# Ten of fourteen hidden tiles of a gated MLP's first half put on a seven-product scheme, with partial sums kept on chip and a new order of all steps

## The chip, the cores and the metric

The kernel runs on one core of a Trainium2 chip. The metric is the device time of one execution in microseconds; several executions of the same program are timed and their median is given. The core's engines run side by side, each through its own instructions in order: PE (the matrix engine), DVE and ACT (element-wise work, DVE on two tensors, ACT on one), POOL (here it issues transfers that add to what is already there) and SP (it issues the other transfers). Transfers run on 16 DMA engines. Matmuls write to PSUM, eight banks of 128 x 512 fp32 values.

## The reference

All tensors are fp32. x has 2048 rows of 512.

```python
def _A_ref(x, w_r, w_i):                       # a spectral filter
    X = rfft2(x)                               # over rows and columns
    return irfft2(X * (w_r + 1j * w_i))
def _B_ref(x, w1, b1, w2, b2):                 # an MLP, 512 -> 1792 -> 512
    h = gelu(einsum("bsd,df->bsf", x, w1) + b1)
    return einsum("bsf,fd->bsd", h, w2) + b2
g = sigmoid((x * gate_w).sum(-1, keepdims=True))
out = g * _A_ref(x, ...) + (1 - g) * _B_ref(x, ...)
```

## The kernel before

**The MLP** is cut into 14 tiles f of 128 hidden columns and four chunks c of 512 rows. The chunks 0 and 1 are the first half (`CA`, letter A in the new code), 2 and 3 the second half (`CB`, B). Each fp32 operand is split into a high part and a low part (ACT copies the rounded high part, DVE subtracts it), and a product is three fast matmuls: high by high, high by low, low by high. So a tile (f, c) takes 4 x 3 = 12 matmuls of 512 columns for its first product, and 4 x 3 for its second (four output tiles q).

- The first half is done by `mlp(p, c)`, plainly: `ph` (12 matmuls into one bank), gelu by ACT in the bank, `split` into `g..h` and `g..l` (ACT copy, DVE difference), then `down` and `keep`.
- The second half is done by `fast(p)` with a seven-product scheme (Winograd's form of Strassen's): two f tiles by two chunks, each with its K of 512 cut in two, would be eight products of six matmuls; it takes seven (42 matmuls in place of 48 for two f and two c). It needs sums of weight halves (`spread_w`: seven tiles `wa0h`, `wa0l`, `wash`, `wasl`, `wath`, `watl`, `wa1` for each pair u of f tiles, by ACT, DVE and one adding transfer) and sums of x halves (`early_x`, `spread_x`, `put`, `less`: seven forms), and three copies (ACT) and two sums (DVE, with `five`) between the products. Its banks are `nu` and `ux`; matmuls add onto values that ACT has copied into `ux`.
- `down` multiplies by w2 into a bank `po` (`poB`) for a group of f tiles, in three groups for the first half (`PASS_A`) and four for the second (`PASS_B`). `keep` copies each bank to SBUF by ACT and sends it to a DRAM tile `bacc[c]`: the first group with a store, the later ones with a transfer by POOL that adds in DRAM.
- w2 tiles come by `halve` (load, ACT copy, ACT negated copy, adding transfer by POOL); for f from 10 on (`KEPT`) the split tiles of the first half are stored in DRAM (`ws`) and read back in the second. The plain w1 tiles come by `load_w`.

**The filter** is a two-dimensional Fourier transform. `forward(j)`, 16 times: two DVE sums and differences, fp32 matmuls `pd` over columns (one extra column pair gives the gate's dot product, read by DVE reductions), split into `zb`, matmuls `py` into two banks, ACT copy `pys`, a DVE sum and a DVE difference, ACT copies to `y`. Then `stage1`, `filt(q0)` and `stage4` are radix-4 steps on DVE, with the filter's weights between (`wf`, its edge columns mended by a DVE instruction with `rev`). `inverse(c, h)` goes back: `sw`, `pq`, fp32 matmuls `pz`, split into `zb`, matmuls `pa` into two banks, DVE sums. For the first half it loads the partial sums from `bacc`, multiplies by the gate (`ba`), and adds them on the way out; for the second half `last` subtracts the bank of the last group from y and writes the result. The gate is spread over partitions into `gb`.

**The order.** Each step is added to a graph with the buffers that it reads and writes. `ORDER` is a list, written out, of all steps; each engine issues its own in that order, and SP's and POOL's transfers are issued in it too. `SLOTS` says which slot of SBUF or which bank each buffer takes. PSUM was in two pools of four banks (`pf`, `pm`). Steps wait for each other by semaphores where they share a buffer.

The start: ten idle matmuls on zeros (`none`) and ten small ones fill PE until the first x and w1 arrive.

Of the kernel before, what the change touches and what calls it, by code (L numbers as in the profile page):

```python
# [23 lines left out]
PASS_A = (range(0, 5), range(5, 10), range(10, 14))  # L24
PASS_B = (range(0, 4), range(4, 6), range(6, 10), range(10, 14))
# [94 lines left out]
PSUM = ("pf", "pm")  # L120

ORDER = """
# [1153 lines left out]
```

## Time and profile before

| | us |
|---|---|
| median of 3 runs | 363.61 (363.47 to 363.66) |
| the profiled execution | 364.53 |
| its span, first to last instruction | 362.6 |
| PE busy | 356.9 (98%) |
| DVE busy | 330.1 (91%) |
| ACT busy | 254.2 (70%) |
| POOL busy | 70.3 (19%) |

In the rows of the profile `L982` is a line of the kernel, the names before and after the arrow are the tile written and the tiles read, `x16` is how many, then the busy time in us and the mean of one in ns; behind the last bar stands how long the engine was idle just before and what ended that. PEld is the loading of weights into PE, which overlaps the matmuls. All matmuls but those of `fast` have the helper's line L416. The chain of waits is the work that ended last, followed back from the last instruction.

### The profile page before, as it was taken

Reading aid. Unit: us, or ns where it says so; the run is one execution under the profiler, and the core shown is the slowest. Engines: PE = TensorE matmul, PEld = TensorE weight load, DVE = VectorE, ACT = ScalarE, POOL = GpSimd, SP = SyncE. Lnnn points to the kernel's source line nnn. Section 1 sums busy time; section 2 is a strip of 40 time slices with the busy share of each in tenths; the row PEclk is TensorE's granted clock in tenths of the full one; section 3 lists DMA queues with packets and bytes.
Section 4 is the critical chain, followed back from the end, with each engine's and each line's share of the span. In section 5 each row is a group of like instructions: output and inputs, shape, how many; then the busy total and the mean of one; then the engine's idle time right before and its main releaser. Section 6 shows DMA issues by size and latency. Waiting matters only on the chain.

```text
span 362.6 us, 5730 instructions
## 1 busy us (share of the span) xinstructions
PE 356.9 (98%) x1812; PEld 303.1 (84%) x1812; DVE 330.1 (91%) x745; ACT 254.2 (70%) x471; POOL 70.3 (19%) x91
## 2 busy tenths in 40 slices
PE   8999999999999999999999999999999999999995
PEld 6888898898878788888888888888888888889885
DVE  3879999989988899999999899999988889999995
ACT  4796487989988623266566775999999988676200
POOL 1121000111021241111024420010323221113220
PEclk9999999999999999999999999999999999999999
DMA  6999868579768599998988997074869658489878
GB/s 243 339 343 210 280 200 240 115 190 211 212 131 231 135 251 182 283 297 227 266 173 136 185 142 226 32 197 104 149 104 163 111 95 177 122 207 210 210 182 244
DMA packets 46494, 70.34 MB, mean 194 GB/s; under 512 B 5376, under 2 KB 19200, under 8 KB 46464
## 3 DMA queue, kind: packets, MB, share of 16 engines
q1 hardware_dynamic: 34592, 48.93, 42.6%
q0 software_dynamic: 11440, 20.72, 37.0%
q10 hardware_dynamic: 432, 0.33, 0.3%
q8 instruction: 14, 0.23, 0.3%
q14 instruction: 16, 0.13, 0.1%
HBM read 48.32 MB, written 19.41 MB: 187 GB/s over the span
## 4 chain that ended last, share of the span: by engine, by line
PE 91%; DMA 4%; SPq 1%; ACT 1%; DVE 1%; issue 1%; DVEq 0%; ACTq 0%
PE poB L416 21%; PE po L416 20%; PE ph L416 17%; PE ux L1090 11%; PE nu L1090 8%; PE pd L416 4%; PE pz L416 4%; PE py L416 3%; PE pa L416 3%; DMA bacc<-o 3%; DMA war<-in_w 1%; ACT gb L1199 0%; SPq L877 0%; SPq L657 0%; DVE mxl L560 0%
## 5 line engine op out<-in xcount | busy, mean ns | idle before, releaser
L904 ACT ACTIVATE ph<-ph,b1t 128x512 f32<-128x512 f32 x28 | 18.3, 655 | 15.0 <-PE ph L416 15.0
L407 POOL DMA_DIRECT2D bacc<-oB x16 | 14.2, 908 | 53.5 <-ACT oB L982 52.8
L803 ACT ACTIVATE sw<-y,al 64x512 f32<-64x512 f32 x32 | 22.9, 721 | 1.2 <-DVE y L669 0.7
L407 POOL DMA_DIRECT2D bacc<-o x16 | 14.9, 993 | 41.0 <-ACT o L982 38.2
L765 DVE TENSOR_TENSOR m<-y,wf 128x514 f32<-128x514 f32 x32 | 21.5, 691 | 0.2
L982 ACT ACTIVATE o<-po 128x512 f32<-128x512 f32 x16 | 9.3, 598 | 16.8 <-PE po L416 16.8
L632 ACT ACTIVATE y<-pys 64x257 f32<-64x257 f32 x32 | 13.4, 418 | 6.4 <-DVE pys L629 5.7
L416 PEld LDWEIGHTS pz<-tg,pq 128*128 128x128 f32 x128 | 16.8, 191 | 1.2
L416 PE MATMUL pd<-cf,w 128*128 128x129 f32 x128 | 17.8, 274 | 0.0
L416 PEld LDWEIGHTS pd<-cf,w 128*128 128x128 f32 x128 | 16.8, 190 | 0.8
L1090 PE MATMUL nu<-xf,wa0h 128*128 128x512 f32 x56 | 17.5, 393 | 0.0
L416 PE MATMUL pz<-tg,pq 128*128 128x128 f32 x128 | 17.2, 274 | 0.0
L416 PE MATMUL py<-zb,tf 128*128 128x258 f32 x96 | 17.1, 294 | 0.0
L810 DVE SCALAR_TENSOR_TENSOR pq<-y,al,sw 128x256 f32<-128x256 f32 x32 | 14.8, 479 | 0.9 <-ACT sw L803 0.7
L416 PEld LDWEIGHTS py<-zb,tf 128*128 128x128 f32 x96 | 14.3, 190 | 1.1
L416 PEld LDWEIGHTS pa<-zb,ci 128*128 128x128 f32 x96 | 13.9, 188 | 1.4
L416 PE MATMUL pa<-zb,ci 128*128 128x256 f32 x96 | 14.9, 283 | 0.0
L607 DVE TENSOR_TENSOR zb<-pd,zb 128x256 fp32r<-128x256 f32 x32 | 12.7, 419 | 0.6 <-ACT zb L604 0.5
L604 ACT ACTIVATE zb<-pd 128x256 fp32r<-128x256 f32 x32 | 12.0, 384 | 1.5 <-PE py L416 0.9
L574 DVE TENSOR_TENSOR w<-eo 128x256 f32<-128x256 f32 x32 | 12.8, 419 | 0.3
L571 DVE TENSOR_TENSOR eo<-xf 128x256 f32<-128x256 f32 x32 | 12.9, 419 | 0.0
L823 DVE TENSOR_TENSOR zb<-pz,zb 128x512 fp32r<-128x512 f32 x16 | 10.9, 687 | 2.1 <-ACT zb L822 2.1
(700 smaller groups left out, 1273.4 us busy)
## 6 DMA issues: line engine op xcount, KB each, us to landing
wf<-in_wf SPq DMA_DIRECT2D x16, 257.0 KB
bacc<-o POOLq DMA_DIRECT2D x16, 256.0 KB, 6.2
bacc<-oB POOLq DMA_DIRECT2D x16, 256.0 KB, 5.0
xf<-in_xt SPq DMA_DIRECT2D x14, 256.0 KB
wr<-in_w SPq DMA_DIRECT2D x14, 256.0 KB, 4.6
tf<-tf SPq DMA_DIRECT2D x16, 192.0 KB, 4.5
bacc<-o SPq DMA_DIRECT2D x8, 256.0 KB, 5.0
ba<-bacc SPq DMA_DIRECT2D x8, 256.0 KB, 8.4
```

The source lines that it names most:

```text
L407: return add("pool", 2.3 * kb / 340, 3.4, lambda: nc.gpsimd.dma_start(dst(), src(), accum_op=ALU.add), reads, writes, rank)
L416: pe.matmul(ps, w, x, start=start, stop=stop)
L571: v(lambda s=s, op=op: vec.tensor_tensor(eo.ap()[:, s], x.ap()[:, 0:2], x.ap()[:, 2:4], op=op), 256, [x], [(eo, s)], feed)
L574: v(lambda s=s, op=op: vec.tensor_tensor(w.ap()[:, s], eo.ap()[:, :, 0], eo.ap()[:, :, 1], op=op), 256, [eo], [(w, s)], feed)
L604: a(lambda c=c: act.activation(segs(xh, c), both(c), AF.Copy), 256, [ps[c]], [(xh, c)], 0)
L607: v(lambda c=c: vec.tensor_tensor(segs(xl, c), both(c), segs(xh, c), op=ALU.subtract), 256, [ps[c], (xh, c)], [(xl, c)], 0)
L632: a(lambda o=o, i=i: act.activation(Y[j].ap()[o:o + HP, 1], pys.ap()[i:i + HP, 1], AF.Copy), 257, [(pys, 1)], [(Y[j], 1 + k)], 0, more=0.1)
L765: v(lambda mk=mk, k=k, y=y, w=w: vec.tensor_tensor(mk.ap(), y.ap(), w.ap()[:, k:k + 1, :ND].to_broadcast([P, 2, ND]), op=ALU.mult), 514, [ ...
L803: a(lambda sw=sw, y=y, o=o, i=i: act.activation(sw.ap()[o:o + HP], y.ap()[i:i + HP, ::-1, :HD], AF.Copy, scale=al.ap()[i:i + HP, 0:1]), 51 ...
L810: v(lambda sw=sw, pq_=pq_, y=y, j=j, k=k, op=op: vec.scalar_tensor_tensor(pq_.ap()[:, k], y.ap()[:, k, :HD], al.ap()[:, 1 + j:2 + j], sw.a ...
L904: a(lambda: act.activation(ps.ap(), ps.ap(), AF.Gelu_apprx_tanh, bias=b1t.ap()[:, f:f + 1]), 600, [b1t], [ps]).table = "gelu"
L1090: pe.matmul(o.ap(), w(wi, e), FX[j].ap()[:, xi, e], start=first, stop=k == 5, skip_group_check=not start)
```

## The change

- The first half's `f` 4 to 13 go by the seven-product scheme too (`seven("A", u, G)` for five pairs u); only `f` 0 to 3 stay plain (`plain`). The x of the first half is split straight into the scheme's forms (`split_x`), and `spread_x("A")` makes the other four.
- The groups of f are now four in each half: 0-3, 12-13, 4-7, 8-11 for A and 8-11, 12-13, 0-3, 4-7 for B.
- The seven weight tiles of the five pairs are stored in DRAM (`wu`, 35 stores of 256 KB) when A makes them, and B reads them back (35 loads) and doesn't make them again.
- Partial sums stay in SBUF (`SUM`, eight tiles at a time): from the second group on ACT copies the sum into the bank, the matmuls add onto it, and ACT copies it back. The adding transfers into `bacc` are gone; `bacc` is written once for A, after the gate product, and is added by POOL to the inverse's result. B's last group goes from the bank through two DVE instructions to the output.
- Both products of a `py` step, and of a `pa` step, share one bank: ACT copies the first, the second adds onto it, and DVE gets the difference as -2 x first + sum. The gate's dot products are copied out by ACT and summed once; the edge columns come ready from DRAM and are copied by ACT.
- All eight banks are one pool. `ORDER` and `SLOTS` are new throughout.

The diff, cut to what is spoken of:

```diff
-PASS_A = (range(0, 5), range(5, 10), range(10, 14))
-PASS_B = (range(0, 4), range(4, 6), range(6, 10), range(10, 14))
+GROUPS = (range(0, 4), range(12, 14), range(4, 8), range(8, 12)), (range(8, 12), range(12, 14), range(0, 4), range(4, 8))
+PLAIN = 4
...
+    wu = {u: one(f"su{u}", [P, 7, D], pool=dp, parts=7) for u in range(PLAIN // 2, NF // 2)}
...
     def forward(j):
-            v(lambda c=c, o=o: vec.tensor_reduce(o.ap()[:, n:n + 1], ps[c].ap()[:, P:P + 2], ...
+            a(lambda c=c: act.activation(logit.ap()[:, n, c], ps[c].ap()[:, P:P + 2], AF.Copy), ...
...
+        py = bank([P, 512], f"py{j}", "py")
+        for c in range(2):
+            m(lambda c=c: high(c), NE, 2, [t, (xh, c)], [py])
+            m(lambda c=c: low(c), NE, 1, [t, (xl, c)], [py])
+            o, w_ = ((lambda: pys.ap()[:, 0]), (pys, 0)) if c == 0 else ((lambda: Y[j].ap()[:, 0]), (Y[j], 0))
+            a(lambda o=o: act.activation(o(), py.ap()[:, :ND], AF.Copy), 257, [py], [w_])
+        v(lambda: vec.scalar_tensor_tensor(pys.ap()[:, 1], pys.ap()[:, 0], -2.0, py.ap()[:, :ND], op0=ALU.mult, op1=ALU.add), ...
...
+    def spread_w(s, u):
+        if s == "B" and u in wu:
+            for i, n in enumerate(TS):
+                dma(lambda i=i, n=n: raw(T[n].ap(), wu[u].ap()[:, i]), 256, [(wu[u], i)], [T[n]])
+        else:
...
+            if s == "A":
+                for i, n in enumerate(TS):
+                    dma(lambda i=i, n=n: sp.dma_start(wu[u].ap()[:, i], T[n].ap().bitcast(F32)), 256, [T[n]], [(wu[u], i)])
...
+    def down(p, c, fs, G):
+        end = p == len(GROUPS[0]) - 1
+        for q in range(NQ):
+            if p == 0:
+                SUM[c, q] = buf("w", [P, 4 * P], F32, f"s{c}{q}", cls="s")
+            o = SUM[c, q]
...
+                ps = bank([P, size], f"po{p}_{c}{q}{n.start}", "po", full=not tail, onto=p > 0)
+                if p:
+                    a(lambda ps=ps, n=n, o=o: act.activation(ps.ap(), o.ap()[:, n], AF.Copy), size, [o], [ps])
+                for f in fs:
...
+                if p == 0:
+                    a(lambda ...: act.activation(o.ap(), ps.ap(), AF.Identity, bias=b2t.ap()[:, q:q + 1]), 600, [b2t, ps], [o])
+                elif not end:
+                    copy(o, ps)
+                elif c in CA:
+                    copy(o, ps, scale=-1.0)
+                    v(... gate product on o ...)
+                    dma(... o to bacc[c] ...)
+                else:
+                    last(c, q, ps, n, tail)
+
+    def last(c, q, ps, n, tail):
+        for k, i in enumerate(some):
+            v(lambda ...: vec.scalar_tensor_tensor(t.ap()[:, s], gb..., 1.0, ps.ap()[:, s], op0=ALU.subtract, op1=ALU.mult), ...
+            v(minus_, ...)
...
...
+    def group(s, p):
+        if s == "A" and fs[0] < PLAIN:
...
+        else:
+            for u in range(fs[0] // 2, fs[-1] // 2 + 1):
+                seven(s, u, G)
```

More of the change, by code (lines that the diff above doesn't have):

```diff
@@ L332, in schedule @@
             for b in s.bufs:
-                last = held.setdefault((b.tag, b.slot), b)
-                assert last is b or last.left == 0
+                last = held.get((b.tag, b.slot))
+                assert last is b or last is None or last.left == 0
+                assert last is b or not b.onto or last.full
                 held[b.tag, b.slot] = b
@@ L418, in prods, with mm, onto, copy @@
-    def prods(ps, ah, al, bh, bl, first, last):
-        mm(ps, ah, bh, first, False)
-        mm(ps, ah, bl, False, False)
-        mm(ps, al, bh, False, last)
+    def mm(ps, w, x, start, stop, **more):
+        pe.matmul(ps, w, x, start=start, stop=stop, **more)
+    def onto(ps, w, x):
+        mm(ps, w, x, False, False, skip_group_check=True)
     def bcast(ap, *ns):
         return bass.AP(tensor=ap.tensor, offset=ap.offset, ap=[list(ap.ap[0]), *[[0, n] for n in ns], list(ap.ap[1])])
+    def copy(o, i, n=512, scale=1.0):
+        a(lambda: act.activation(o.ap(), i.ap(), AF.Copy, scale=scale), n, [i], [o])
@@ L444, in tile_kernel @@
     b1t = one("b1t", [P, NF])
-    rev = one("rev", [P, NJ, 2, 2])
-    b22 = one("b22", [P, 2, NQ], parts=2)
-    b2t, nb2 = (View(b22, i, 1, lambda t, i=i: t[:, i]) for i in range(2))
+    b2t = one("b2t", [P, NQ])
     al = one("al", [P, 1 + NJ])
-    logit = one("logit", [P, NJ], parts=NJ, pool=sa)
-    gate = one("gate", [P, NJ], parts=NJ, pool=sa)
+    logit, edges = (buf("lg", [P, NJ, 2, 2], F32, n, k, sa) for n, k in (("logit", 2 * NJ), ("edges", 1)))
+    gate = one("gate", [P, NJ], pool=sa)
     gb = buf("xhl", [P, 4, 4 * P], F32, "gb", parts=4, cls="gb")
@@ L453, in tile_kernel @@
     Y = [View(yy, 3 * j, 3, lambda t, j=j: t[:, j]) for j in range(NJ)]
-    bacc = [one(f"bacc{c}", [P, NQ, 4, P], pool=dp, parts=2 * NQ) for c in range(4)]
+    bacc = [one(f"bacc{c}", [P, NQ, 4, P], pool=dp, parts=2 * NQ) for c in CA]
     ws = {(f, k): one(f"sb{f}{k}", [P, D], pool=dp) for f in range(KEPT, NF) for k in "hl"}
+    wu = {u: one(f"su{u}", [P, 7, D], pool=dp, parts=7) for u in range(PLAIN // 2, NF // 2)}
     gsc = one("gsc", [P, NJ], pool=dp)
@@ L611, in forward, with high @@
-        py = [buf("pm", [P, 512], F32, f"py{j}{c}", pool=pp, cls="py") for c in range(2)]
+        for c in range(2):
+            v(lambda c=c: vec.tensor_tensor(segs(xl, c), both(c), segs(xh, c), op=ALU.subtract), 256, [ps[c], (xh, c)], [(xl, c)])
+            a(lambda c=c: act.activation(logit.ap()[:, n, c], ps[c].ap()[:, P:P + 2], AF.Copy), 2, [ps[c], (xh, c)], [(logit, 2 * n + c)],
+              more=0.1)
+        py = bank([P, 512], f"py{j}", "py")
         pys = t2k(f"pys{j}", cls="pys", parts=2)
-        def s_high(c):
+        def high(c):
@@ L825, in inverse, with part @@
-        ps = [buf("pf", [P, 2, 2 * P], F32, f"pa{c}{h}{ft}", pool=pp, cls="pa") for ft in range(2)]
-        def part(ft, p, z, k, first, last):
-            mm(ps[ft].ap()[:, k], CI[0].ap()[:, k, p, ft], z.ap()[:, ft, k].rearrange("p a b -> p (a b)"), first, last)
+              512, [ps, (zh, n)], [(zl, n)])
+        ps = bank([P, 2, 2 * P], f"pa{c}{h}", "pa")
+        def part(ft, p, z, k):
+            mm(ps.ap()[:, k], CI[0].ap()[:, k, p, ft], z.ap()[:, ft, k].rearrange("p a b -> p (a b)"), ft == p == k == 0 and z is zh, False,
+               skip_group_check=True)
@@ L884, in load_w @@
         src = (w1 if n == "a" else w2)[f]
-        own = n == "a" and f < 6
+        own = n == "a" and f < 2
         t = buf("w", [P, D], F32, f"w{n}r{f}", cls=n + "t", parts=2 if first else 1) if own else None
@@ L893, in load_w @@
             dma(lambda: sp.dma_start(t.ap(), src), 256, [], [t])
[L894 removed]
+            copy(h, t)
         if own:
@@ new lines, in plain, with prod, up, some @@
+    def plain(c, f):
+        xs = [FX["A", k] for k in (("11", "21") if c == 0 else ("12", "22"))]
+        ps = bank([P, 512], f"ph{c}_{f}", "ph", full=True, parts=3)
+        def prod(k, l, q, n, start, stop):
+            mm(ps.ap()[:, n], W["a", f][k].ap()[:, q * P:(q + 1) * P], xs[q // 2].ap()[:, l, q % 2, n], start, stop)
+        if c or f > 1:
+            def up():
+                for q in range(NQ):
+                    for k, l in ((0, 0), (0, 1), (1, 0)):
+                        prod(k, l, q, slice(None), q == k == l == 0, q == NQ - 1 and k == 1)
+            m(up, 512, 12, [*W["a", f], *xs], [ps])
+        else:
+            def some(k, l, js, qs, start, stop):
+                for q in qs:
+                    prod(k, l, q, slice(js.start * P, js.stop * P), start and q == 0, stop and q == NQ - 1)
+            for j in range(0 if f else 2):
+                for k in range(2):
+                    add("pe", 0.24 if j else 0.45, 0.25, lambda j=j, k=k: some(0, 0, range(j, j + 1), range(2 * k, 2 * k + 2), j == 0, False),
+                        [(W["a", f][0], k), *piece(xs[k], 0, range(2), [j])], [(ps, 0), *([] if j or k else [(ps, 2)])])
+            for n in range(2):
+                for k, l in ((0, 0), (0, 1), (1, 0))[0 if n or f else 1:]:
+                    js = range(2 * n, 2 * n + 2)
+                    m(lambda n=n, k=k, l=l, js=js: some(k, l, js, range(NQ), n == k == l, n == k == 1), 256, 4,
+                      [W["a", f][k], *([] if n == 0 else [(ps, 2)] if k == l else [(ps, 0)]), *[p for x in xs for p in piece(x, l, range(2), js)]],
+                      [(ps, n), *([(ps, 2)] if n == k == l else [])])
+        gelu(ps, f)
+        return split(f"g{c}_{f}", ps)
@@ new lines, in last, with minus_ @@
+    def last(c, q, ps, n, tail):
+        ys = [Y[c + 8 * h + 4 * (q // 2)] for h in range(2)]
+        dst = out[c][:, q].rearrange("p a b -> p (a b)")
+        t = buf("w", [P, ps.shape[1]], F32, f"t{c}{q}{n.start}", parts=2, cls="t")
+        some = range(0, ps.shape[1], P) if tail and n.start else (0,)
+        for k, i in enumerate(some):
+            w = ps.shape[1] // len(some)
+            o = [(t, k)] if len(some) > 1 else [t]
+            s = slice(i, i + w)
+            v(lambda s=s, i=i, w=w: vec.scalar_tensor_tensor(
+                t.ap()[:, s], gb.ap()[:, c, n.start + i:n.start + i + w], 1.0, ps.ap()[:, s], op0=ALU.subtract, op1=ALU.mult), w, [gb, ps], o)
+            def minus_(s=s, i=i, w=w):
+                if ps.shape[1] == 4 * P:
+                    y = yy.ap()[:, c + 4 * (q // 2)::8, q % 2, :2 * P]
+                    x = t.ap().rearrange("p (a b) -> p a b", a=2)
+                else:
+                    y, x = ys[n.start // (2 * P)].ap()[:, q % 2, i:i + w], t.ap()[:, s]
+                vec.tensor_tensor(x, y, x, op=ALU.subtract)
+            v(minus_, w, [(y, q % 2) for y in (ys if not tail else ys[n.start // (2 * P):][:1])], o)
+            if k:
+                add("act", 0.4, 2.6, lambda s=s, i=i, w=w: act.dma_start(dst[:, n.start + i:n.start + i + w], t.ap()[:, s]), o, [])
+            else:
+                dma(lambda s=s, i=i, w=w: sp.dma_start(dst[:, n.start + i:n.start + i + w], t.ap()[:, s]), w / 2, o, [])
@@ L1032, in spread_w, with spread_x, raw_x, to @@
-    def spread_w(u, late):
+    def spread_x(s):
+        cs = CA if s == "A" else CB
+        new_forms(s, ("t1", "t2", "t3", "t4") if s == "A" else ("11", "t1", "t2", "21", "t3", "22", "t4"))
+        def raw_x(k, n, e):
+            x = buf("w", [P, 4 * P], F32, f"xb{s}{k}{n}{e}", cls="xb")
+            dma(lambda: sp.dma_start(x.ap(), xc[cs[n], 2 * k + e]), 256, [], [x])
+            return x
+        for e in range(2):
+            b00, b01, b11, b10 = (raw_x(k, n, e) for k, n in ((0, 0), (0, 1), (1, 1), (1, 0)))
+            def to(k, x):
+                if k[0] == "t" or s == "B":
+                    put(FX[s, k], e, x)
+            to("11", b00)
+            less(b00, b01, b00)
+            to("t1", b00)
+            less(b01, b11, b01)
+            less(b00, b11, b00)
+            to("t2", b00)
+            to("21", b10)
+            to("t3", b01)
+            to("22", b11)
+            less(b10, b10, b00)
+            to("t4", b10)
@@ L1179, in tile_kernel, with seven, times, emit @@
-    BY_ACT = NORD[0:]
+    def seven(s, u, G):
+        cs = CA if s == "A" else CB
+        A = spread_w(s, u)
+        N = [bank([P, 512], f"nu{s}{u}{k}", "nu", full=True) for k in range(2)]
+        X = [bank([P, 512], f"ux{s}{u}{k}", "ux", full=True, onto=True) for k in range(2)]
+        def times(o, i, j, start):
+            bs, w = A[i]
+            x = FX[s, j]
+            def emit():
+                k = 0
+                for e in range(2):
+                    for wi, xi in ((0, 0), (0, 1), (1, 0)):
+                        mm(o.ap(), w(wi, e), x.ap()[:, xi, e], start and k == 0, k == 5, skip_group_check=not start)
+                        k += 1
+            m(emit, 512, 6, [*bs, x], [o])
+        def plus(o, i, t):
+            v(lambda: vec.tensor_tensor(o.ap(), i.ap(), t.ap(), op=ALU.add), 512, [i, t], [o])
+        def done(ps, i, n):
+            gelu(ps, 2 * u + i)
+            G[cs[n], 2 * u + i] = split(f"g{cs[n]}_{2 * u + i}", ps)
+        times(N[0], "11", "11", True)
+        times(N[1], "s1", "t1", True)
+        copy(X[0], N[0])
+        five = buf("t2k", [P, 512], F32, f"five{s}{u}", cls="five")
+        copy(five, N[1])
+        times(X[0], "s2", "t2", False)
+        times(N[0], "12", "21", False)
+        done(N[0], 0, 0)
+        copy(X[1], X[0])
+        times(X[0], "s3", "t3", False)
+        times(X[1], "s4", "22", False)
+        plus(X[1], X[1], five)
+        done(X[1], 0, 1)
+        plus(N[1], X[0], five)
+        done(N[1], 1, 1)
+        times(X[0], "22", "t4", False)
+        done(X[0], 1, 0)
@@ L1206, in tile_kernel @@
     own_rows()
-    early_x()
-    for p in range(len(PASS_A)):
-        for c in CA:
-            mlp(p, c)
+    group("A", 0)
+    spread_x("A")
+    for p in range(1, len(GROUPS[0])):
+        group("A", p)
     for q0 in range(4):
@@ L1215, in tile_kernel @@
         for h in range(2):
-            inverse(c, h, False)
+            inverse(c, h)
     for c in CA[::-1]:
         stage4(c)
-    spread_x()
-    for p in range(len(PASS_B)):
-        fast(p)
+    spread_x("B")
+    for p in range(len(GROUPS[1])):
+        group("B", p)
         if p < 2:
             for h in range(2):
-                inverse(CA[1 - p], h, True)
+                inverse(CA[1 - p], h)
     order = g.schedule([int(n) for n in ORDER.split()], iter([int(n) for n in SLOTS.split()]))
@@ L1257 @@
     rows = (P * np.arange(NJ)[:, None] + KROW) % S
-    wrev = wf[back[rows]][:, :, :, [0, HD]].transpose(1, 0, 2, 3)
+    wrev = np.stack([wf[r][:, :, :, [0, HD]].transpose(1, 0, 2, 3) for r in (rows, back[rows])], 1)
     wf = wf[rows][:, :, :, FORD]
```

563 lines of the change are left out of this document (187 added, 376 removed), and 195 rows, old and new, of tables (ORDER, SLOTS).

## The prediction

> **What bounds the kernel now.** I read the header of the page first, then what PE waited for, then the busy time by stage, and last the groups of ACT, DVE and the DMA queues.
>
> ```profile
> span 362.6 us, 5730 instructions
> PE 356.9 (98%) x1812; PEld 303.1 (84%) x1812; DVE 330.1 (91%) x745; ACT 254.2 (70%) x471; POOL 70.3 (19%) x91
> ...
> PE none L416 <- DVE zero L484: 1.1, 1, 1.1
> PE ph L416 <- DVE wa0h L891: 0.7, 1, 0.7
> PE ph L416 <- DVE wa0l L896: 0.2, 1, 0.2
> PE po L416 <- ACT o L982: 0.2, 1, 0.2
> ```
>
> The four waits are all that PE waited for: 2.2 us, nearly all at the start. PE works from 1.05 us to the end, so PE's instruction stream is the time. A busy PE isn't a PE at its peak, so the price of a matmul comes from runs of them in the chain of waits, not from their single spans:
>
> ```profile
> 130.18 2.72 PE ph L416 x12
> ...
> 143.78 7.48 PE po L416 x33
> ```
>
> 2.72/12 and 7.48/33 both give 0.227 us for one 512-column matmul, back to back. The stages (columns PE, PEld, DVE, ACT, POOL busy, clock, DMA share, GB/s) show how much room the others have:
>
> ```profile
> 0.00:20.00 20.00, 18.04 (x97) 15.60 (x97) 12.25 (x29) 13.19 (x24) 3.50 (x14) 1.00 0.88 302
> 20.00:100.00 80.00, 80.00 (x462) 70.21 (x461) 73.76 (x208) 65.26 (x143) 8.63 (x10) 1.00 0.82 218
> 260.00:300.00 40.00, 40.00 (x213) 34.40 (x212) 35.49 (x74) 37.95 (x68) 11.54 (x14) 1.00 0.71 117
> ```
>
> From 20 to 100 us ACT is busy 82%, DVE 92%, and from 260 to 300 us ACT even 95%, while PE isn't stopped once. A busy ACT does no harm as long as it keeps ahead of PE.
>
> **The change, part by part.**
>
> *Fewer matmuls.* Before, the first products of the first half take 28 tiles (f, c) of 12 matmuls: 336. After, four f stay plain (8 tiles, 96 matmuls) and five pairs of f take seven products of six matmuls: 210. 306 against 336: 30 fewer, 30 x 0.227 = 6.80 us off PE. The second half has its 7 x 42 already; the 672 matmuls of the second products, the transforms and the fillers stay in number. With no new wait all of it is gained.
>
> *The tail.* After the last matmul there are now, for each of the two 128-wide pieces, two DVE instructions in place of one, and the last DMA waits for all four.
>
> ```profile
> 358.72 0.28 PE L416 MATMUL poB<-g_13h,wb13lb 128*128 128x256 f32 x1
> 359.03 0.49 DVE L1164 TENSOR_TENSOR oB<-y,poB 128x128 f32<-128x128 f32 x2 [0.68 <-PE poB L416]
> ```
>
> Two take 0.49 us, so four take twice that: +0.49 us, in full on the path. At the head the two halves of the first weight tile move ahead of the first x tile on SP's queue; PE's wait of 0.7 us for them is the most that it can give, and the x that is now later can take it back. I put it at 0, with 0.7 as the low end.
>
> *ACT.* These are the rows that I price with (mean of one behind the busy time):
>
> ```profile
> L904 ACT ACTIVATE ph<-ph,b1t 128x512 f32<-128x512 f32 x28 | 18.3, 655 | 15.0 <-PE ph L416 15.0
> L632 ACT ACTIVATE y<-pys 64x257 f32<-64x257 f32 x32 | 13.4, 418 | 6.4 <-DVE pys L629 5.7
> L604 ACT ACTIVATE zb<-pd 128x256 fp32r<-128x256 f32 x32 | 12.0, 384 | 1.5 <-PE py L416 0.9 <-PE pd L416 0.5
> L982 ACT ACTIVATE o<-po 128x512 f32<-128x512 f32 x16 | 9.3, 598 | 16.8 <-PE po L416 16.8
> L625 ACT ACTIVATE pys<-py 128x257 f32<-128x257 f32 x16 | 6.1, 379 | 0.3 <-PE py L416 0.2
> L979 ACT ACTIVATE o<-po,b 128x512 f32<-128x512 f32 x8 | 5.5, 689 | 3.4 <-PE po L416 3.4
> L1096 ACT ACTIVATE ux<-nu 128x512 f32<-128x512 f32 x7 | 4.1, 585 | 3.3 <-PE nu L1090 3.3
> L559 ACT ACTIVATE mxh<-xf 128x512 fp32r<-128x512 f32 x6 | 3.7, 632 | 0.0
> L555 ACT ACTIVATE mxh<-xf 128x256 fp32r<-128x256 f32 x3 | 1.1, 411 | 2.4 <-DMA xf<-in_x0g 1.3 <-DMA xf<-in_xt 1.1
> L1186 ACT ACTIVATE gate<-logit 128x16 f32<-128x16 f32 x1 | 0.2, 215 | 0.0
> 2.95 0.20 ACT L486 ACTIVATE gate<-zero 128x1 f32<-128x1 f32 x1
> ```
>
> Added: 49 copies of a sum from SBUF into PSUM. No row shows that pair of memories; PSUM to PSUM takes 0.585, SBUF to SBUF 0.632, I take 0.60 for the middle: 29.4 us. 8 more stores of sums (56 against 48) at 0.598: 4.8. 15 copies inside the five new pairs at 0.585: 8.8. 8 more x forms at 0.632: 5.1. x split in half tiles, 15 at 0.411 in place of 6 at 0.632 and 3 at 0.411: 1.1. 16 copies of py at 0.379: 6.1. 32 logit copies and 16 edge copies, a few columns each, at 0.20: 9.6. 8 copies of 256 columns in the inverse, at most 0.411: 3.3. Removed: 16 copies of plain first weights at 0.632: 10.1. Net 58 us and about 140 instructions. Row means overcount, for ACT's instructions overlap: the 143 of 20:100 sum to 72.8 us by their rows in that window (from y's 32 at 418 ns to the gate's one at 215), but the stage shows 65.26 (0.053 us less for each); the 68 of 260:300 sum to 43.0 and show 37.95 (0.074 less). So ACT grows by some 49 us, from 254 to 303, 85% of the new span. On average that fits, and DVE proved that 91% can.
>
> It doesn't lie evenly. I numbered the steps as the code adds them (2098) and walked down the new order list. Up to step 722, the copy of a sum into the bank of poA1_11 (second group of f, first half), ACT has 246 steps; PE's next step on that bank has 104.4 us of PE work ahead of it, which with the 2.2 us of waits makes 106.6 us. The 246 are 71 copies of 512 columns (44.0 us), 16 gelus (10.5), 8 with the bias b2 (5.5), 116 of 256 or 257 columns (45.7), 32 of two columns (6.4) and three with a table load (4.5): 116.5 us by row means, less 246 x 0.053 to 0.074: 98.3 to 103.5. In the first 20 us ACT is idle 6.8 us (20 less 13.19), waiting for the first loads, and still will be. So ACT is through at 105.1 to 110.3 us if it never waits again: between 1.5 us early and 3.7 late. Should it be idle as in its densest stage (2.05 us of 40, over some 90 us), 4.6 more. A delay of PE there comes back nowhere, since PE has no gap later. The ends are 0 and 8.3 us; I take 3.2: the middle of the overlaps (1.1 late) and not quite half of the idle time (2.1), for the queue is full and yet in order, with instructions that wait for DVE in it. By the list, ACT needs about 40 us for the 56 us of PE work from there to 160 us, and keeps ahead for the rest.
>
> The Trainium skill (ScalarE: Activation LUTs, What ACT_TABLE_LOAD costs) gives an ACTIVATE 186 ns and 0.833 ns per element, 93 ns more with a pointer operand, and lets back-to-back ones overlap by 93 ns. An estimate by that page is 95 us for the same 246, 101 us with the idle start, ahead of PE's 106.6; the sum would then be 357.3 us. The overlap of 0.053 to 0.074 us in this trace is smaller, and I keep to the trace.
>
> *DVE.* Gone: 32 small reductions, 16 adds of 257 columns, 16 edge products, 8 adds in the inverse, 8 gate products on gelu's input; the last stage has 14 instructions of 512 columns and six small in place of 8 of 512 and 31 of 256. Added: 10 sums in the new pairs, 16 for the x forms.
>
> ```profile
> L608 DVE TENSOR_REDUCE logit<-pd 128x1 f32<-128x2 f32 x16 | 2.4, 152 | 0.0
> L626 DVE TENSOR_TENSOR y<-py,pys 128x257 f32<-128x257 f32 x16 | 6.6, 420 | 1.0 <-ACT pys L625 0.5 <-PE py L416 0.5
> L760 DVE SCALAR_TENSOR_TENSOR wf<-wf,rev 128x4 f32<-128x4 f32 x16 | 2.5, 159 | 0.0
> L854 DVE TENSOR_TENSOR u<-pa,od 128x512 f32<-128x512 f32 x8 | 5.5, 689 | 0.2
> L1105 DVE SCALAR_TENSOR_TENSOR ux<-gb,ux 128x512 f32<-128x512 f32 x4 | 2.8, 690 | 0.0
> L1140 DVE SCALAR_TENSOR_TENSOR bb<-gb,bb 128x512 f32<-128x512 f32 x8 | 5.4, 686 | 0.2 <-DMA bb<-bacc 0.2
> L1144 DVE TENSOR_TENSOR y<-y,bb 128x256 f32<-128x256 f32 x16 | 6.4, 421 | 0.0
> L1171 DVE TENSOR_TENSOR oB<-y,poB 128x256 f32<-128x256 f32 x15 | 5.7, 417 | 0.4 <-PE poB L416 0.3
> L1099 DVE TENSOR_TENSOR nu<-ux,five 128x512 f32<-128x512 f32 x7 | 4.9, 695 | 1.4 <-PE ux L1090 1.3
> ```
>
> 4.9 + 6.7 + 2.5 + 5.5 + 5.5 + 7 + 2.8 (four weights at 0.69) off, 7.0 + 11.0 (both at 0.69) + 1.2 (x in halves) on: about 13 us less, 317 in all. DVE's cover is no worse than now; 0 on the path. If it ran late, the low halves of gelu would be first to hold PE.
>
> *Waits added.* Both products of a transform step now share one bank: PE's second pair waits until ACT has copied the first, and behind it stands all of PE's queue. The list puts other work between in most places, so 0 if ACT is in time; it is one more way in which a late ACT reaches PE, and the price is in the 3.2. The copies into PSUM read sums stored long before by ACT itself; they can only be late through the queue.
>
> *DMA, SP, POOL.* 35 stores of weight sums and 35 loads of 0.262 MB come in (18.4 MB), 24 transfers of partial sums and 10 weight loads go (8.9 MB), and POOL's accumulating transfers fall from 79 to 42.
>
> ```profile
> q1 hardware_dynamic: 34592, 48.93, 42.6%
> q0 software_dynamic: 11440, 20.72, 37.0%
> ...
> SPq L848 <- PE poB L416: 15.8, 2, 14.0
> ```
>
> By these shares per MB, 58.4 MB and 11 MB make 51% + 20%, against 80% now. Not a bound. SP issues the stores in order and each waits for its tile, with loads of later weights and x behind; in the last row SP stood 14 us behind one wait without PE noticing, so 0. If loads came too late, a weight tile of B would be first, seen as a PE wait on a DMA.
>
> *Sum.* -6.80 + 0.49 + 3.2 = -3.1 us. The profiled execution took 364.53 us (span 362.6); so 361.4 for one like it. It lies 0.92 above the median of the runs, 363.61; against that, **360.5 us**.
>
> **The rivals.**
>
> *ACT keeps ahead.* For it: 260:300, at 95% without a stop. Against: 80 us at such a load in a row occur nowhere in the trace. It gives 363.6 - 6.8 + 0.5 = 357.3; with the head's 0.7, 356.6.
>
> *ACT becomes the bound and takes back more than is saved (slower).* Place: 20 to 110 us. The saving left after the tail is 6.3 us; at 1.1 us late by load alone, it decides at 5.2 us of further ACT idle time before step 722, 5.9 for more than 0.2% slower. In 20:100 ACT is now idle 14.7 us of 80. For it: that number, if a third or more of that idle time stays. Against: those are waits of an ACT ahead of its work, 15.0 us of them for ph in the row above over the whole kernel. The likely price there is a time of 365; if all stayed it would be some 373.
>
> *A gap that costs twice.* The ten first fillers show PE at a lower pace:
>
> ```profile
> L416 PE MATMUL none<-zero 128*128 128x512 f32 x10 | 4.6, 645 | 1.1 <-DVE zero L484 1.1
> ```
>
> 4.6 us for ten, against 2.3 at 0.227. If ACT's delay came as one long gap and PE had to warm up again, 2.3 us more: 362.8. The stalls should be many and short, for each bank has its own copy. The Trainium skill (TensorE: Matmul & The Clock Gate, HAM oscillation) sets the gap that throttles at about 3.4 us; here the longest wait is 1.1 us and the granted clock 1.00 throughout, so no run here shows it in mid kernel.
>
> **How the numbers follow.** 0.2% (0.7 us) is about what a measurement of this kernel can tell from no change. Forecast, ACT late by 1 to 5.5 us: 0.46, faster. ACT ahead, below 358.3: 0.22, faster. Late by 5.6 to 7.0: 0.12, no change. Slower: 0.17 for ACT as the bound, 0.03 for the gap that costs twice on top of a late ACT. Faster 0.68, same 0.12, slower 0.20. The range goes from the first rival's end, 356.8, to 365.5, where ACT is late by 8.3; that leaves some 0.15 out. The likeliest case alone is 358.3 to 362.8.
>
> **What would show it.** Right: 30 fewer PE matmuls and the first products at 0.227; ACT above 95% from 20 to 110 us and PE waits on ACT (poA1, ux, py) of 2 to 5 us in all there, none after 160 us; ACT near 303, DVE near 317 us; POOL's queue at half its share; last matmul to last DMA 0.5 us longer. Wrong: a PE that waits for DVE or DMA, or later than 160 us; ACT with idle time in 20:110 while PE waits; small copies far off 0.2 us; copies into PSUM far off 0.6.

## The result and the profile after

The changed kernel takes 388.9 us (median of four, 388.5 to 390.9) against 363.6 for the kernel before on the same chip: 1.069 times as long, with an interval of 1.063 to 1.075. The forecast was 360.5 us. The profiled execution took 390.9 us (a span of 389.1), 2.0 above the median. Yet the instructions came out nearly as counted. The head of the page and the DMA queues, after:

```profile
span 389.1 us, 5714 instructions
PE 362.3 (93%) x1782; PEld 299.5 (77%) x1782; DVE 324.6 (83%) x672; ACT 299.8 (77%) x614; POOL 40.5 (10%) x54
...
q1 hardware_dynamic: 38752, 58.36, 45.0%
q0 software_dynamic: 7136, 10.79, 18.5%
```

There are 30 fewer matmuls; ACT has 299.8 us (303 forecast), POOL's queue 18.5% of the DMA engines (20%). What is new is that PE waits. Columns: what waited for what, us in all, times, longest:

```profile
PE po L409 <- ACT po L927: 6.3, 5, 3.3
PE uxB L409 <- DMA wB<-su: 3.0, 1, 3.0
PE py L409 <- ACT pys L622: 2.0, 2, 1.7
PE uxA L409 <- ACT uxA L418: 1.3, 1, 1.3
...
PE py L409 <- ACT logit L605: 0.9, 2, 0.5
PE pd L409 <- ACT logit L605: 0.6, 1, 0.6
```

By stages (the columns of the prediction's table of stages; the clock is the third from the end):

```profile
20.00:140.00 120.00, 111.80 (x568) 91.09 (x567) 102.88 (x221) 104.88 (x258) 11.98 (x14) 1.00 0.72 200
140.00:260.00 120.00, 113.51 (x485) 92.69 (x484) 108.35 (x204) 85.23 (x159) 10.31 (x12) 0.97 0.72 206
260.00:380.00 120.00, 117.19 (x620) 97.94 (x619) 95.15 (x195) 98.00 (x172) 13.86 (x13) 1.00 0.43 107
```

PE stands still in every stage, while ACT, DVE and the DMA engines are all less than full. To see how much, I took the start of every matmul in each trace and compared its distance to the next with what that shape takes in an unbroken run (0.227 us for 512 columns, 0.12 for 256; 0.111 for each of the two records of a 128-column fp32 matmul). The sum of these is PE's work, the rest is lost (a slower clock's share included):

| us | before | after | r1_full | r5_margin | r6_best |
|---|---|---|---|---|---|
| PE's work | 351.6 | 344.8 | 344.6 | 344.6 | 344.8 |
| lost between matmuls | 6.1 | 36.3 | 19.8 | 9.3 | 11.3 |
| last matmul's start to the end | 3.9 | 7.0 | 6.4 | 5.7 | 4.4 |
| span of the profiled run | 362.6 | 389.1 | 371.9 | 360.6 | 361.5 |

(The first matmul starts at 1.05 us in all.) After against before: -6.8 of work, as forecast; +30.2 lost and +3.1 at the end, where 3.2 and 0.49 were forecast. By the place of the matmul, 2.1 of the 30.2 lie before 20 us, 12.4 between 20 and 140, 10.3 between 140 and 260 and 5.5 after that. The rest of this text looks for the 30.2. The three kernels on the right run the same steps as the changed kernel in other orders; they come below. The profiled execution of r6_best took 363.2 us, 1.6 above its median, so its column looks worse than the kernel is. One execution of r1_full, of 593.8 us at a granted clock of 0.56, is in none of its numbers.

One of the two longest stalls, in order of time (here and in the other stretches below, only the rows that are spoken of):

```profile
173.51 0.39 PE L409 MATMUL po<-g_8h,wb8l 128*128 128x512 f32 x1
174.53 0.60 ACT L418 ACTIVATE g_10h<-nuA 128x512 fp32r<-128x512 f32 x1 [4.47 <-DMA su<-wA0l]
176.55 0.60 ACT L927 ACTIVATE po<-s 128x512 f32<-128x512 f32 x1
176.68 0.32 SPq L875 DMA_DIRECT2D sb11h<-wb11h  x1
177.20 0.79 PE L409 MATMUL po<-g_8h,wb8h 128*128 128x512 f32 x1 [3.30 <-ACT po L927]
177.79 0.63 PE L409 MATMUL po<-g_8l,wb8h 128*128 128x512 f32 x1
```

g_10h takes the SBUF slot of wA0l. That tile's store to DRAM, among the tile's users (its duration in ns as shortest, median and longest, then first and last start):

```profile
L1046 SPq DMA_DIRECT2D su<-wA0l x1: 397/397/397, 166.0 to 166.0; - x1
```

It was issued at 166.0 and freed the slot 8.5 us later, among loads, stores and three adding transfers. ACT stood 4.47 us for it, the copy of a sum into the next bank came behind, PE stood 3.30 us, and SP, which had a store waiting for an ACT copy, issued nothing meanwhile. Then the matmuls start 0.43 to 0.59 us apart, where an unbroken run has 0.227.

The other long one, at 254.54 us, is the 3.0 us for wB above. Its load takes the slot of a partial sum `s`; the store of that sum was issued at 245.10, and the load only at 251.59:

```profile
245.10 0.32 SPq L943 DMA_DIRECT2D bacc<-s  x1
251.59 0.32 SPq L406 DMA_DIRECT2D wB<-su  x1
254.54 0.70 PE L409 MATMUL uxB<-xBt,wB 128*128 128x512 f32 x2 [3.00 <-DMA wB<-su]
```

Among SP's waits is the one for the landing of this store (in all, times, longest):

```profile
SPq L406 <- DMA bacc<-s: 8.4, 2, 6.1
```

All eight stores at L943 together:

```profile
DMA to landing us min/median/max: 2.8/4.6/6.4
```

They took 2.8 to 6.4 us from issue to landing, for the same 256 KB.

### The profile page after: what moved, and what is told of

Read it like the earlier page. It is cut to its first block, busy times and chain, and to the rows that moved or that the text cites. A ratio compares the mean times of both kernels' runs of the same rounds, so it can differ in the third digit from the quotient of the medians.

```text
span 389.1 us, 5714 instructions
## 1 busy us (share of the span) xinstructions
PE 362.3 (93%) x1782; PEld 299.5 (77%) x1782; DVE 324.6 (83%) x672; ACT 299.8 (77%) x614; POOL 40.5 (10%) x54
## 3 DMA queue, kind: packets, MB, share of 16 engines
q1 hardware_dynamic: 38752, 58.36, 45.0%
q0 software_dynamic: 7136, 10.79, 18.5%
## 5 line engine op out<-in xcount | busy, mean ns | idle before, releaser
L927 ACT ACTIVATE po<-s 128x512 f32<-128x512 f32 (+1 forms) x49 | 28.6, 588 | 3.5 <-DVE t L957 3.1
L418 ACT ACTIVATE s<-po 128x512 f32<-128x512 f32 x40 | 23.4, 592 | 4.3 <-PE po L409 4.1
L409 PE MATMUL py<-zb,tf 128*128 128x258 f32 x96 | 20.1, 303 | 2.9 <-ACT pys L622 2.0
L409 PE MATMUL pd<-cf,w 128*128 128x129 f32 x128 | 19.6, 280 | 1.3 <-ACT logit L605 0.6
L409 PE MATMUL pz<-tg,pq 128*128 128x128 f32 x128 | 18.4, 277 | 1.1 <-DVE pq L795 0.9
L409 PE MATMUL nuB<-xB,wB0h 128*128 128x512 f32 x56 | 17.7, 397 | 0.2 <-DMA wB0h<-su 0.2
L409 PE MATMUL pa<-zb,ci 128*128 128x256 f32 x96 | 16.6, 289 | 0.6 <-DVE zb L808 0.6
L878 ACT ACTIVATE uxB<-uxB,b1t 128x512 f32<-128x512 f32 x14 | 9.1, 659 | 7.6 <-PE uxB L409 4.2
L409 PE MATMUL uxB<-xBt,wB 128*128 128x512 f32 x42 | 11.4, 408 | 3.0 <-DMA wB<-su 3.0
```

The costliest lines, as they stand in the source:

```text
L409: pe.matmul(ps, w, x, start=start, stop=stop, **more)
L418: a(lambda: act.activation(o.ap(), i.ap(), AF.Copy, scale=scale), n, [i], [o])
L927: a(lambda ps=ps, n=n, o=o: act.activation(ps.ap(), o.ap()[:, n], AF.Copy), size, [o], [ps])
```

## The experiments

Four were aimed at one suspect each in the changed kernel, seven run its steps in orders made anew, and the last takes one suspect out of the best of these.

**e1_lru: other slots, same order.** In `schedule`, for the two pools `w` and `t2k`:

```diff
+ life[b] = lo, i, i + (150 if self.steps[n].eng == "sp" and i > lo else 0)
...
+ b.slot = min((k for k in was if was[k][0] < lo), key=lambda k: was[k][1])
```

> The order of all steps stays as in the changed kernel; only the SBUF slots are dealt anew: a tile of the 46-slot pool and of the 7-slot pool takes the free slot that was left longest ago, and a slot left by a store counts as left 150 steps later. Theory S (slots are handed on while a store out of them still waits or runs): the 4.5 us and 2.1 us that ScalarE stood for a store of wA0l go, and with them the 3.3 us of TensorE at 177 us and the slower clock after it (about 1.6 us), and the wait of t for an output store at the end (2.3 us): 388.9 - 7 = 382 us. Theory Q (SyncE's queue is late as a whole) and theory A (ScalarE has too much to do, or trades banks with VectorE too tightly, ahead of 140 us): 387 to 389 us, the same waits under other names.

Measured: 395.8 us, 7 more than the changed kernel; ratio to before 1.088 [1.086, 1.091]. Theory S in this simple form fell. PE's waits in it:

```profile
PE po L422 <- ACT po L940: 5.6, 7, 2.0
PE po L422 <- DMA wb11l<-in_w: 2.5, 1, 2.5
PE nuB L422 <- DMA wB0l<-su: 2.1, 1, 2.1
```

The waits of 3.3 and 3.0 us are gone, and others stand in their place, two of them for loads. The way the slots are dealt was not the cause by itself. Read off the lists, the slot of a tile that is stored to DRAM is taken by the next tile a median of 27 steps after the store in the changed kernel (55 such slots, 30 of them within 30 steps; 2098 steps take 389 us, so 30 take some 5.6 us on average). It is 70 in the kernel before (3 of 31 within 30), 62 in r5_margin and 54 in r6_best, but 97 in e1_lru, which is the slowest of these.

**e2_nowu: no stores of weight sums.**

```diff
- dma(lambda i=i, n=n: sp.dma_start(wu[u].ap()[:, i], T[n]...), 256, [T[n]], [(wu[u], i)])
+ add("sp", 0.0, 0.0, lambda: None, [], [(wu[u], i)])
```

> Left out: the 35 stores of the weight sums to DRAM; the second half loads as many tiles of 256 KB from another place, so its products of the seven-product pairs are of other numbers. Theory S or Q: the backlog of the stores, the slots that wait for them and SyncE's issues of them (35 of 257) are gone, so the gap at 177 us goes and the loads at 254 us come earlier: 376 to 381 us. Theory A: what is lost ahead of 140 us stays, and only the gap at 177 us goes: 383 to 386 us.

Measured: 381.3 us, ratio 1.048 [1.045, 1.051]: 7.6 us less, at the edge of what S or Q said. So 35 transfers that I had priced at nothing cost 7.6 us in this list; some 18 us above the kernel before stay. By the working of the table above, the loss between 140 and 260 us falls from 10.3 to 5.0 us, and that between 20 and 140 us only from 14.0 to 10.4.

**e3_pool: SyncE relieved.**

```diff
- dma(lambda t=t, j=j: sp.dma_start(t.ap(), ti_d[j]), 64, [], [t])
+ add('pool', 64 / 340, 2.8, lambda t=t, j=j: nc.gpsimd.dma_start(t.ap(), ti_d[j]), [], [t])
```

and likewise the stores of `out[c]` from w.

> The 16 loads of tg and the 8 stores of the first half's output are issued by GpSimd's queue instead of SyncE's. Theory Q: the load of wB at 251.6 us no longer stands behind loads of tg that wait for TensorE, and the last stores not behind stores that wait for an adding DMA: the 3.0 us at 254.5 us with its slower clock (about 2 us) and some 2 us of the end go, 382 to 383 us. Theory S alone: 386 to 389 us. If GpSimd's adding DMAs come to stand behind these loads, 390 us or more.

Measured: 408.7 us, ratio 1.124 [1.117, 1.132], the third outcome. What waited on GpSimd, and what then waited on PE:

```profile
POOL tg L781 <- DVE wBtl L1028: 37.8, 1, 37.8
POOL tg L781 <- PE pz L409: 31.7, 5, 11.4
...
PE po L409 <- DVE g_7l L460: 5.1, 1, 5.1
```

A load of tg waits for a slot, and every adding transfer behind it waits too. It only moved the queueing to another queue, so whether SyncE's queue is the cause is left open by this run.

**e4_noonto: without the copies into PSUM.**

```diff
- a(lambda ps=ps, n=n, o=o: act.activation(ps.ap(), o.ap()[:, n], AF.Copy), size, [o], [ps])
+ add("act", 0.0, 0.0, lambda: None, [o], [])
```

> Left out: the 49 copies of a partial sum from SBUF into PSUM; the groups of products after the first start new sums, so the output lacks the earlier groups. ScalarE has 49 x 0.588 = 28.8 us less to do, 16 or so of these copies ahead of 140 us. Theory A with ScalarE's load as the limit: the 16 us that are lost between 20 and 140 us shrink by 8 to 10, and the 3.3 us before a copy at 177 us go, 372 to 377 us. Theory S: the copies only show what holds ScalarE up; 384 to 388 us.

Measured: 383.7 us, ratio 1.057 [1.053, 1.062]: 5.2 us less, at the edge of what S said and far from A's 372 to 377. With ACT at 274.5 us in place of 299.8, PE still waits 2.7 us for wB, 1.9 for pys and 1.3 for uxA. Each of the four runs stays over 17 us above the kernel before, so none of these suspects alone was the cause; what they all keep is the order.

**r1_full, r2_nobank, r3_nodma: the same steps in other orders.** For these I wrote a replay of the trace. Each step keeps its measured duration; a step starts when its engine is free and what it reads, overwrites or takes the slot of is done, with the delays that the traces show (0.05 us from ACT or DVE to PE, 0.03 to 0.04 from PE to these and between them). Fed with the changed kernel's own list and the waits from the code alone, it ended far too early. What it lacked was seen by comparing each step's start with the trace. First, banks: two engines that read one PSUM bank do it one after the other in this program, in the order of the list, the second waiting for the first, though the step graph has no such dependence. Here ACT's copy of two logit columns has all it needs, but DVE's read of the same bank is listed ahead of it, and that stands behind six other instructions on DVE:

```profile
38.78 0.68 DVE L460 TENSOR_TENSOR g_3l<-ph,g_3h 128x512 fp32r<-128x512 f32 x1
39.38 0.41 DVE L604 TENSOR_TENSOR zb<-pd,zb 128x256 fp32r<-128x256 f32 x1
39.83 0.17 ACT L605 ACTIVATE logit<-pd 128x2 f32<-128x2 f32 x1 [2.26 <-DVE zb L604]
40.06 0.38 PE L409 MATMUL pd<-cf,w 128*128 128x129 f32 x1 [0.64 <-ACT logit L605]
```

The Trainium skill (PSUM — Partial Sum Buffer, PSUM bank collisions raise a hardware error) says that accesses of two engines to one bank have to be kept apart by semaphores, by the bank and not by the address; this trace agrees, with the 2.26 us of that row. Second, transfers: they share the DMA engines. By the page's rows a packet of the adding queue takes 18.5% x 389.1 x 16 / 7136 = 0.161 us, one of SP's queue, as long in bytes, 45.0% x 389.1 x 16 / 38752 = 0.072. With both in, the replay came to 392. A search then moved steps and slots at random and kept what made the replay end earlier. The edit is the list alone:

```diff
- ORDER = """ 0 495 15 113 23 497 496 498 499 14 ...
+ ORDER = """ 0 15 13 14 34 38 16 26 500 33 37 ...
```

> The same 2098 steps and instructions as in the changed kernel; only their order and the slots are made anew, by a search over a replay of the trace in which every instruction keeps its measured duration, a bank that ScalarE and VectorE both read is read by one at a time in the order of the list, and transfers share the DMA engines (0.74 us of them for 256 KB, 2.0 us for an adding one). The replay puts the changed kernel's own list at 392 us (measured span 389) and this one at 352. Theory O (the seven-product scheme costs nothing beside its instructions; the list of the steps was made for transfers and hand-offs that the chip doesn't give): 352 to 358 us. Theory A (ScalarE's added copies are what holds TensorE up, in any order): 380 us or more.

> As r1_full, but the search took a bank to be readable by ScalarE and VectorE at once. If that rule is a cost that the list has to know of, 5 to 10 us over r1_full (the full replay says 358.8 + 1.8 = 360.6 us); if the rule is nothing, the same as r1_full.

> As r1_full, but the search took every transfer to land after the time that it needs alone (2.5 us for 256 KB, 3.9 us for an adding one), however many are under way. If the list's trouble is that transfers queue behind each other, and what waits for a store's slot with them, 375 to 390 us (the full replay says 384.8 + 1.8); if transfers have room in any order, as 45% and 18.5% of the DMA engines' time suggest, the same as r1_full.

Measured against before: r1_full 1.0221 [1.0196, 1.0245], some 371.5 us; r2_nobank 1.0255 [1.0218, 1.0292], 373.0; r3_nodma 1.0632 [1.0568, 1.0696], 385.6. Theory A fell: with every copy still on ACT the same instructions run 17 us faster. A list that counts on transfers landing after a fixed time loses 14 us against one that lets them share the engines, as forecast. That is most of the 17 us by which the changed kernel is behind r1_full. Its code gives each transfer such a fixed time too (2.8 us, 3.4 for an adding one, in `dma` and `acc`), as does that of the kernel before; that its list was made from these is not shown. The bank rule made no difference that these runs show, where 5 to 10 us were forecast. And the forecast of 352 to 358 for r1_full missed by 14. I put it down to transfers that land later still than that replay had them, which the next runs try, and to gaps that cost more than their length:

```profile
178.20:181.60 3.40, 1.42 (x7) 0.90 (x6) 3.40 (x8) 1.98 (x4) 0.00 (x0) 1.00 1.05 403
181.60:185.00 3.40, 3.40 (x10) 2.63 (x9) 0.95 (x2) 1.12 (x2) 0.00 (x0) 0.50 0.55 197
```

PE waited 2.0 us in the first of these windows of r1_full, for a load of wB0h; in the second its clock is 0.50 throughout.

**r4_margin, r5_margin: later landings, and the clock.**

> The changed kernel's steps and instructions again, in a list searched anew. The replay now takes from the traces so far: 2.2 us of the DMA engines per us of an adding transfer, landings 0.9 us (SyncE) and 1.3 us (GpSimd) later than their median, and TensorE's clock in windows of 3.41 us, at half speed in a window after one that was busy for less than 46%. It gives 356.4 us for this list. Theory O (late transfers were what the lists lacked): 358 to 364 us, TensorE's idle time halved against r1_full. If transfers land later than any such margin, or the loss comes from something that the replay has no part for, 370 us or more as r1_full.

> As r4_margin, from another start of the search; the replay gives 357.3 us. The two should agree within 3 us if the replay holds what matters; if they differ by more, the rest is luck of single transfers.

Measured: 363.9 us, ratio 1.0021 [1.0000, 1.0043], and 362.6 us, 0.9981 [0.9972, 0.9990]. They agree within 3 us, and both lie in the forecast of 358 to 364. The loss between matmuls is 14.6 us in r4's profiled execution (366.8 us, 2.9 above its median) and 9.3 in r5's, against 19.8 in r1_full's. With the margins the changed kernel's instructions run as fast as the kernel before. Several things went into the replay at once here (landings, the price of adding transfers, the clock), so their shares aren't told apart.

**r6_best, r7_nobank: searched on, and the bank rule once more.**

> The changed kernel's steps and instructions, in a list searched on from r5_margin's, with the first 8 us and the end given their nominal landings; the replay gives 355.1 us with 3.0 us of TensorE idle, where it gave r5_margin 357.0 with 5.1 (measured: span 360.6, 362.6 us). Theory O: 360 to 362 us, under the kernel before by 1.5 to 3 us. If what is left is the luck of single transfers, 362 to 364 us.

> As r5_margin (same start, same time of search, same margins for transfers), but the search took a bank to be readable by ScalarE and VectorE at once. With the transfers out of the way, what such a list loses is seen at 2 us or more if the rule matters: 365 to 369 us. If a list loses nothing by not knowing it, 362 to 364 us as r5_margin.

Measured: r6_best 361.6 us, ratio 0.9958 [0.9936, 0.9981], as forecast and 0.4% faster than the kernel before. r7_nobank 367.6 us, 1.0110 [1.0094, 1.0126], as forecast by the rule: 5.0 us more than r5_margin (4.7 by the ratios). No list of the kernel before was searched in this way, so how the two compare after equal search is open; it has 6.1 us between its matmuls to win. In these lists, one that doesn't know of the bank rule loses some 5 us; it is one list of each kind, and two searches with the rule, r4 and r5, came out 1.3 us apart. In r7 ACT waits five times as in the row above:

```profile
ACT logit L605 <- DVE zb L604: 5.0, 5, 1.3
```

In r6_best PE hardly waits any more (head, waits, two stages):

```profile
PE 353.3 (98%) x1782; PEld 298.2 (83%) x1782; DVE 318.0 (88%) x672; ACT 296.8 (82%) x614; POOL 40.5 (11%) x54
...
PE pd L409 <- DVE w L571: 1.5, 1, 1.5
PE none L409 <- DVE zero L477: 1.1, 1, 1.1
PE pd L409 <- DVE cf L523: 0.8, 1, 0.8
PE po L409 <- ACT po L927: 0.6, 1, 0.6
...
20.00:140.00 120.00, 119.93 (x626) 102.16 (x625) 115.09 (x252) 110.92 (x270) 13.61 (x16) 1.00 0.78 222
140.00:260.00 120.00, 120.00 (x531) 98.51 (x529) 115.32 (x225) 97.22 (x178) 10.32 (x12) 1.00 0.71 207
```

Between 20 and 140 us the same engines do more per microsecond than in the changed kernel (ACT 110.92 against 104.88, DVE 115.09 against 102.88, DMA 0.78 against 0.72): they weren't too slow there, they waited for each other.

**r8_noonto: what ACT's added copies cost in a good list.** The edit of e4_noonto on r6_best.

> r6_best's list and slots; left out are the 49 copies of a partial sum from SBUF into PSUM, so the groups after the first start new sums and the output lacks the earlier groups. It prices what the prediction put at 3.2 us (ScalarE's added work): if ScalarE's load still holds TensorE in this list, 2 to 4 us under r6_best; if the list hides it, within 0.7 us of r6_best (one wait of 0.6 us for such a copy is left in it).

Measured: 359.4 us, ratio 0.9885 [0.9868, 0.9901]: 2.2 us under r6_best. So ACT's load still holds PE a little, as the first outcome said. Where isn't settled: in the two profiled runs most of the difference lies in the first 20 us, in which no such copy stands, and r6_best's has a window at half clock there. That window isn't all of it, for the six executions of r6_best at a granted clock of 0.999 or more still have a median of 361.4 us.

## Why the prediction was wrong

*Fewer matmuls: right.* -6.8 us in the trace's work, -6.80 forecast.

*The tail: 3.1 us in place of 0.49.* Here the cause is a slot again. t takes that of an earlier output tile whose store is late:

```profile
382.08 0.28 PE L409 MATMUL po<-g_7h,wb7l 128*128 128x256 f32 x1
383.39 0.69 DVE L957 SCALAR_TENSOR_TENSOR t<-gb,po 128x512 f32<-128x512 f32 x1 [2.34 <-DMA out<-t]
```

The two added instructions alone cost what was said: r6_best, without that wait, has 4.4 us after the last matmul's start, 0.5 more than before.

*ACT: the size was about right, the stage and the reason weren't.* 303 us forecast, 299.8 measured; r8_noonto takes somewhat over half of the added work out of a good list (ACT 272.5 us against 296.8) and gains 2.2 us, where I put 3.2 for all of it. But ACT was to be above 95% busy from 20 to 110 us, with PE waiting 2 to 5 us for it; by the row of 20 to 140 it is 87% busy while PE stands. It waited itself, for DVE, for transfers and for slots.

*DVE: near the measured time in a list without stalls* (318.0 in r6_best, 317 forecast; 324.6 after), but by a slip: the terms of the working come to 15.7 us off, not 13, which makes 314. It was 0 on the path either way.

*Waits added, put at 0: wrong.* I argued that the list puts other work between. It does so by a graph that has no order between two reads of a bank. Ignoring the rule cost some 5 us in a list (r7_nobank against r5_margin); how much of the 30 it is in the changed kernel's own list no run tells.

*DMA, SP and POOL, put at 0: with the waits above, the step that failed.* It was read off shares of busy time, 51% + 20% against 80%, and off one row in which SP stood 14 us without harm. The share did fall, to 63.5%. But a mean share says nothing of when a transfer lands. A store that lands late stops the ACT or DVE instruction or the load that takes its slot, and with it all that stands behind on that queue; both long stalls above are of this kind. The step did say what a failure would look like, a weight tile of B that PE waits for, and that wait of 3.0 us is there. e2_nowu prices the 35 stores at 7.6 us in the changed kernel's own list, and r3_nodma against r1_full prices lists without and with that knowledge at 14 us. How the rest of the 30.2 splits stays open: between 20 and 140 us most of it stays without the stores, and PE waits there for ACT, which itself waits for DVE (some 5 us) as well as for transfers (some 4).

*The gap that costs twice, given 0.03: it happened twice in mid kernel.*

```profile
173.40:176.80 3.40, 0.50 (x3) 0.08 (x1) 1.64 (x3) 2.27 (x5) 0.00 (x0) 1.00 0.43 162
176.80:180.30 3.50, 3.10 (x7) 2.48 (x8) 3.50 (x8) 2.76 (x6) 0.00 (x0) 0.51 0.76 241
252.00:255.30 3.30, 0.76 (x3) 0.67 (x4) 2.00 (x4) 0.63 (x1) 0.00 (x0) 1.00 0.66 178
255.30:258.70 3.40, 3.40 (x10) 2.64 (x9) 0.58 (x1) 1.87 (x4) 0.00 (x0) 0.51 0.00 1
```

Each time PE was busy for under a quarter of a window of 3.4 us, and the next window ran at half clock: some 1.7 us each (half of 3.41), on top of the stall.

The rivals all shared the assumption under these steps: that the new list, whatever its engines' load, runs as it was laid out. The list was the part of the change that I did not price at all: in lists searched anew the same steps lose 3.2 us (r5_margin) to 5.2 us (r6_best) more between matmuls than the kernel before, where the changed kernel's own list loses 30.2. The slower rival had the right sign, at a price of 365, for one engine's load; the loss came from many waits in which no engine was full.

## What to carry to other kernels

When a change comes with a new order written out by hand or by a planner, the order is a change of its own: run the removed and added work through the list with measured durations, shared banks, slots and late transfers before counting a saving, or give the list a chance of its own to lose. A mean share of the DMA engines is no cover for a store whose slot is taken again; ask of each store who takes its slot next, how many microseconds later, and what stands behind that instruction. And before dropping a change that came out slower with no engine full, lay its order out again: here the same instructions went from 1.069 to 0.996 of the time before.

## What the runs showed of the hardware

- PE's clock is granted in windows of 3.41 us: up to 380 us the changed kernel's trace has three stretches at half clock, of 3.41 us each, which begin at 9.59, 176.84 and 255.35 us, 49 and 23 times 3.41 apart. A window of r1_full in which PE was busy for 1.42 us (above, 42%) was followed by one at half clock; one of e2_nowu with 1.57 us (48%) was not:

```profile
179.90:183.20 3.30, 1.57 (x7) 1.30 (x8) 2.94 (x6) 1.78 (x4) 0.00 (x0) 1.00 0.45 141
183.30:186.60 3.30, 3.30 (x16) 2.72 (x16) 3.22 (x7) 2.81 (x5) 0.00 (x0) 1.00 0.79 260
```

  So a gap of 2.0 us can be enough. The share alone doesn't decide: at the changed kernel's start a window with PE busy for 2.15 us (6.2 to 9.6 us, small matmuls) was followed by half clock too. The Trainium skill (TensorE: Matmul & The Clock Gate, HAM oscillation) asks for gaps of no more than about 3.4 us; the windows agree, but r1_full differs with its 2.0 us, and the measurement decides.
- An adding transfer holds the DMA engines 2.2 times as long as a plain one of the same bytes (0.161 against 0.072 us for a packet of 1.5 KB; by the page of before it is 2.6 times, 0.188 against 0.071), and a store of 256 KB lands 2.8 to 6.4 us after its issue in one and the same kernel.
- A copy of 128 x 512 from SBUF into PSUM by ACT, which no row of before showed, takes what I took for it (0.60):

```profile
L927 ACT ACTIVATE po<-s 128x512 f32<-128x512 f32 x47 | 27.8, 596 | 2.1 <-DVE t L957 1.7
```
